# Loading half of the q and k blocks earlier and transposing them in another stage

## The chip, the cores and the metric

The kernel runs on one core of one Trainium2 chip. The time is that of the device, in microseconds, as a median of three runs.

## What is computed

Block-decayed linear attention over q, k, v of shape (4, 8, 768, 64), followed by a two-layer network with the activation h - tanh(h). All numbers are float32.

```python
for b in range(nb):                     # blocks of 64 positions
    intra = einsum('bhic,bhjc->bhij', qb, kb) * Dmask[None]
    intra = einsum('bhij,bhjd->bhid', intra, vb)
    inter = einsum('bhid,bhde->bhie', qb * lam_pow[None], kv_state)
    out[:, :, sl] = intra + inter
    kb_dec = kb * rev_pow[None]
    kv_state = lam_block[None, :, None, None] * kv_state + einsum('bhsd,bhse->bhde', kb_dec, vb)
...
x = out.transpose(0, 2, 1, 3).reshape(3072, 512)
h = x @ w_in                            # (3072, 512) x (512, 2048)
g = h - tanh(h)
return g @ w_out                        # (3072, 2048) x (2048, 512)
```

## The kernel before

The 768 positions are cut into six groups of 128 (`g` = 0 to 5). A group holds one chunk for each of the four batches (`b` = 0 to 3), so 512 tokens. For each group the kernel does the attention of its four chunks, then the two layers on its 512 tokens. The attention of group g + 1 is spread over the layers of group g.

Both layers are done with Strassen-like schemes: seven products in place of eight, called 1 to 7. The first layer (`up(g, u, n)`, line 540) runs over four hidden units `u` of 512 columns. The second layer's products are `down_twice(g, n)` (line 797), here called P1 to P7. Each is cut into seven smaller products again, in the order 1, 2, 6, 5, 7, 3, 4, and each smaller product reads one piece of weights (256 KB) which POOL's queue brings from device memory. The pieces go through a ring of seven buffers (`wb`); four pieces of each P5 go into two extra buffers named `rest`.

From group 2 on, one turn of the outer loop is made of these stages:

- The loop over units, with four first-layer products in each (products 3, 7, 6, 4; the 6 of the first two units are done before), and P1 in its second half.
- P2, then the attention products of chunks 0 and 1 of the next group, then P4 and P5. Inside P5 stand the transposes of chunks 2 and 3.
- P6, the attention products of chunks 2 and 3, P7.
- The inner stage: P3, interleaved with products 1 and 2 of the next group's first layer over all units (`inner_steps`, line 623, lines 637 to 651), then product 5.

For groups 2 to 5 q and k are also loaded in blocks of 32 (`load_blocks`, line 164): for two chunks at a time a tile of q and a tile of k, each by 16 transfers of 32 KB on SyncE's queue. The tiles `q_blk` and `k_blk` come from a pool of four buffers, which the two `rest` tiles share in turn. `att_transpose(g, bs)` (line 354) then does for each chunk two VectorE transposes (line 362) and a product of the transposed q with the powers of the decay (line 373).

SyncE's queue carries, for each of these groups, in this order: the blocks of chunks 0 and 1 (32 transfers), the natural k and v of chunks 0 and 1 (`load_natural`, line 143), the blocks of chunks 2 and 3, the natural k and v of chunks 2 and 3. The last group needs no natural k. The dictionary `hold` makes the first transfer of a group wait for a given instruction. In the kernel before that is the copy on ScalarE of the sixth small product of the inner stage (line 641), two groups ahead of the group that uses the data.

Most operations are placed by a scheduler that follows dependencies and a cost model; those inside `keep_in_program_order` and `tied` keep the order of the code.

Of the kernel before, what the change touches and what calls it, by code (L numbers as in the profile page):

```python
# [24 lines left out]
def kernel(  # L25
# [32 lines left out]
    nc = tc.nc  # L58
# [84 lines left out]
    def load_natural(g, b, names):  # L143
        for name, src, bufs in (("q", q, 2), ("k", k, 3), ("v", v, 4)):
            if name in names:
                if (g, b, name) in ((0, 2, "q"), (0, 3, "q"), (0, 3, "k")):
                    x = opool.tile([128, H, D], F32, name=f"{name}_nat", tag="o")
                else:
                    x = (qpool if name == "q" else io).tile([128, H, D], F32, name=f"{name}_nat", tag=name, bufs=bufs)
                rows = src[b, :, ts(g, BLK), :].rearrange("h s d -> s h d")  # L150
                if name == "q":
                    parts = [(nc.sync, x, rows)]
                else:
                    eng = nc.sync if g > 0 else nc.scalar if b == 0 else nc.gpsimd
                    whole_ = {(0, 1, "k"): nc.scalar, (0, 2, "k"): nc.gpsimd}.get((g, b, name), nc.sync)
                    parts = [(eng, x[ts(1 - t, HALF), 4:8], rows[ts(t, HALF), 4:8]) for t in range(2)]
                    parts.insert(2 * (whole_ is nc.gpsimd), (whole_, x[:, 0:4], rows[:, 0:4]))
                for eng, to, of in parts:
                    op = tc.keep_in_program_order(eng.dma_start(out=to, in_=of))
                    if begin.get(eng) is not None:  # L160
                        wait_for(op, begin.pop(eng))
                raw[g, b][name] = x

    def load_blocks(g, half):

        for name, src in (("q", q), ("k", k)):
            x = late["blk"].tile([128, 2 * NP, BLK // 32, 32], F32, name=f"{name}_blk", tag="blk")
            heads = src[ts(half, 2)].rearrange("b (p j) s d -> j s (b p) d", j=2)
            for r in range(BLK // 32):
                for c in range(4):  # L170
                    op = tc.keep_in_program_order(nc.sync.dma_start(
                        out=x[ts(c, 32), :, r], in_=heads[c // 2, g * BLK + 32 * r:g * BLK + 32 * (r + 1), :, ts(c % 2, 32)]))
                    if g in hold:

                        wait_for(op, hold.pop(g))
            for n in range(2):
                raw[g, 2 * half + n][name + "b"] = x[:, ts(n, NP)]

    def load(n):

        while at["loaded"] < min(n, len(chunks)):
            g, b = chunks[at["loaded"]]
            if g < GB:
                raw[g, b] = {}
                load_natural(g, b, "qkv")
                at["loaded"] += 1
                continue
            for b in range(B):  # L190
                raw[g, b] = {}
            nat = "kv" if g < NG - 1 else "v"

            first = (0, 1, 2) if g == GB else ()
            for b in first:
                load_natural(g, b, nat)
            for half in range(2):
                load_blocks(g, half)
                for b in (2 * half, 2 * half + 1):
                    if b not in first:  # L200
                        load_natural(g, b, nat)
            at["loaded"] += B
# [584 lines left out]
    def sums_twice(g, n):  # L787
# [6 lines left out]
            tied(n in (5, 3, 1, 2) or (g, n) == (1, 6), nc.vector.tensor_tensor(dst, x, y, op=op))  # L794
        low[g, n] = (s1, s2, s3, s4)

    def down_twice(g, n):
        a11, a12, a21, a22 = quarter(g, n)
        s1, s2, s3, s4 = low.pop((g, n))
        y, zw = (("ya", "z") if n in (4, 6) else ("yb", "w")) if g == NG - 1 else ("ya", "z") if n in (5, 3) else ("yb", "w")  # L800
        if n < 3:
            y, zw = "att", "w" if n == 2 else "att"
        y, zw = (bank(x, tag, 4 if tag == "att" else 1) for x, tag in (("y2", y), ("zw", zw)))
        y = y[:, 0:128]
        o = res[g, n] = otile(f"q{n}") if n != 2 else late["pool"].tile([128, 512], F32, name="o11", tag="o11", bufs=1)
        for x, a, dst, keep in ((1, a11, y, o[:, 0:128]), (2, a12, zw[:, 0:128], None), (6, s2, y, o[:, 128:256]),
                                (5, s1, zw[:, 256:384], None), (7, s3, y, o[:, 384:512]), (3, s4, zw[:, 128:256], None),
                                (4, a22, y, o[:, 256:384])):
            wb = piece(g, n, x).rearrange("p m c -> p (m c)")
            for u in range(NU):  # L810
                tied(x == STEPS[-1], nc.tensor.matmul(out=dst, lhsT=a[:, u, :], rhs=wb[:, ts(u, 128)],  # L811
                                                      start=x in (1, 2) and u == 0, stop=u == NU - 1,
                                                      skip_group_check=True))
            if keep is not None:
                nc.scalar.activation(keep, dst, AF.Copy)  # L815
            if x == 2 and n > 2:
                tied(n in (5, 7), nc.vector.tensor_tensor(a12, a12, s2, op=AL.subtract))  # L817
            if x != STEPS[-1]:
                yield

        if n in (6, 2):
            yield
        o5 = o.rearrange("q (i c) -> q i c", i=2)[:, :, 128:256]
        tied(n in (6, 2), nc.vector.tensor_tensor(o5, o5, zw[:, 256:384][:, None, :].to_broadcast([128, 2, 128]), op=AL.add))
        tied(n in (6, 2), nc.vector.tensor_tensor(o[:, 0:256], o[:, 0:256], zw[:, 0:256], op=AL.add))
        if n == 6:
            yield
            tc.keep_in_program_order(nc.vector.tensor_tensor(o, o, res[g, 1], op=AL.add))
            for x in (4, 5):
                tc.keep_in_program_order(nc.vector.tensor_tensor(res[g, x], res[g, x], o, op=AL.add))  # L830
        elif n == 2:
            tc.keep_in_program_order(nc.vector.tensor_tensor(o, o, res[g, 1], op=AL.add))
            store(g, 11, o)
        elif n == 7:
            nc.vector.tensor_tensor(res[g, 4], res[g, 4], o, op=AL.add)
            store(g, 21, res[g, 4])
            nc.vector.tensor_tensor(o, o, res[g, 5], op=AL.add)
            store(g, 22, o)
        elif n == 3:
            nc.vector.tensor_tensor(o, o, res[g, 5], op=AL.add)  # L840
            store(g, 12, o)
        yield

    def every(steps):
        for _ in steps:
            pass
# [181 lines left out]
    for g in range(1, NG):  # L1028
# [7 lines left out]
        for u in range(NU):  # L1036
            if g < GI:
                for n in (2, 6, 5, 7, 1, 4, 3):
                    if n != 1:
                        up(g, u, n)  # L1040
                    elif u + 1 < NU:
                        up(g, u + 1, 1)
                    else:
                        every(p_first)
                    if g == 1 and u < 2 and n == 5:
                        sums_in(u + 2)
                    if n == 6:
                        for p in ((), ((1, 0), (1, 1)), ((1, 2), (1, 3), (2, 0)), ((2, 1), (2, 2)))[u]:
                            fine_pieces(*p)
            else:  # L1050
                up(g, u, 3)
                up(g, u, 7)
                if u + 2 < NU:
                    up(g, u + 2, 6)
                else:
                    next(p_first)
                up(g, u, 4)
                if u + 1 == NU:
                    sums_twice(g, 2)
                if u != 2:  # L1060
                    steps(p_first, (2, 1, 0, 2)[u])
                if not last and u < 2:
                    att_transpose(g + 1, (u,))
                elif not last:
                    att_decays(g + 1, (u - 2,))
            if g == GI - 1 and u + 1 < NU:
                inner_weights(u)
            if not last and u > 1 and g < GI:
                run(p0[u - 2:u - 1])
# [34 lines left out]
        sums_once(g, 21, 21, 11)  # L1104
        sums_twice(g, 6)
        every(p5)
        if not last:
            att_decays(g + 1, (2, 3))
        if twice(g, 7):
# [13 lines left out]
        inner_tokens(g + 1)  # L1123
        sums_twice(g, 3)
        p3, pa, pb, pc = (down_twice(g, 3), *(inner_steps(g + 1, n) for n in INNER))
        for _ in STEPS:
            next(p3)
            next(pa)
            next(pb)
        for p in (pa, pb, p3):  # L1130
            every(p)
        for x in STEPS:
# [40 lines left out]
```

## Time and profile before

| | us |
|---|---|
| median of three runs | 652.08 (651.89 to 652.57) |
| profiled execution | 650.99 |
| its span | 649.2 |
| TensorE busy | 641.8 |
| VectorE busy | 499.2 |
| POOL busy | 242.6 |
| mean rate of transfers | 209 GB/s |

The profile is of one execution. A row of the instructions in order of time holds the start in us from the span's start, the duration, the engine (PE is TensorE, PEld its weight loads, DVE VectorE, ACT ScalarE, POOL GpSimd, SP SyncE), the line, the operation, the tile written and the tiles read, and how many instructions the row merges. A bracket holds the idle time of the engine ahead of it and what released it. One float32 matmul of the code shows as two instructions on TensorE. The granted TensorE clock is 1.00 in every window read.

The stages of group 2 lie at 269.05 to 303.45 (loop over units), 303.45 to about 345.5 (P2 to P7), 345.5 to 370.71 (inner stage). Groups 3 and 4 follow at distances of 101.7 and 101.4 us. Group 1's inner stage is at 245.4 to 269.05, and the last group starts its loop at 572.45.

### The profile page before, as it was taken

What the parts mean: (1) busy time and instruction counts of PE and PEld (TensorE: products, weight loads), DVE (VectorE), ACT (ScalarE), POOL (GpSimd) and SP (SyncE); (2) the same over time, 40 slices, a digit from 0 to 9 for tenths busy, and PEclk for the clock granted to TensorE, in tenths of its full rate; (3) what the DMA queues carried; (4) which work ended last, traced back from release to release, by engine and by line L of the source; (5) the groups of instructions that cost most, each with busy time, mean ns of one, the idle gap of its engine ahead of it and who ended that gap; (6) DMA issues with size and microseconds to landing.
All of it is one profiled execution on the core that took longest, in us unless ns stands there. A gap on an engine that the chain in (4) does not pass through costs nothing.

```text
span 649.2 us, 15718 instructions
## 1 busy us (share of the span) xinstructions
PE 641.8 (99%) x6080; PEld 594.7 (92%) x6080; DVE 499.2 (77%) x969; ACT 250.2 (39%) x513; POOL 242.6 (37%) x418
## 2 busy tenths in 40 slices
PE   8999999999999999999999999999999999999998
PEld 7888888888888999989999989999998999998997
DVE  4467989958999895778986678998477997485873
ACT  3686765523221222543223453213453313264210
POOL 6000136767756335203435302443411354411341
PEclk9999999999999999999999999999999999999999
DMA  9869987988979858958757967775967686712575
GB/s 201 214 168 206 247 244 233 382 252 231 276 191 268 242 181 253 220 118 220 247 174 226 248 134 160 230 253 199 237 140 158 199 274 210 233 67 66 159 247 162
DMA packets 160281, 135.79 MB, mean 209 GB/s; under 512 B 128640, under 2 KB 130944, under 8 KB 160208
## 3 DMA queue, kind: packets, MB, share of 16 engines
q0 software_dynamic: 30496, 97.88, 47.8%
q1 hardware_dynamic: 128096, 36.53, 26.6%
q8 instruction: 48, 0.79, 0.5%
q10 hardware_dynamic: 1616, 0.39, 0.3%
q14 instruction: 25, 0.20, 0.1%
HBM read 110.10 MB, written 24.64 MB: 208 GB/s over the span
## 4 chain that ended last, share of the span: by engine, by line
PE 91%; DVE 4%; DMA 2%; ACT 1%; issue 1%; ACTq 0%; SPq 0%; DVEq 0%
PE y L811 17%; PE y L553 17%; PE zw L811 13%; PE h L870 8%; PE y L637 7%; PE z L553 6%; PE acc L900 4%; PE z L637 3%; DMA k_nat<-in_k_dram 2%; PE sp L387 2%; PE op L462 2%; PE w L637 2%; PE kv L408 1%; PE op L433 1%; PE end L856 1%; PE op L473 1%
## 5 line engine op out<-in xcount | busy, mean ns | idle before, releaser
L696 POOL DMA_DIRECT2D wb<-fine x204 | 110.1, 540 | 244.0 <-PE y L811 160.8
L815 ACT ACTIVATE q<-y 128x128 f32<-128x128 f32 x112 | 31.1, 277 | 143.2 <-PE y L811 141.7
L811 PE MATMUL y<-wb,g 128*128 128x128 f32 x584 | 76.5, 277 | 0.2 <-DVE tt L618 0.2
L811 PEld LDWEIGHTS y<-wb,g 128*128 128x128 f32 x584 | 70.5, 192 | 1.2 <-issue 0.4
L870 PE MATMUL h<-xt,w 128*128 128x256 f32 x256 | 57.8, 382 | 0.4 <-DVE w L325 0.4
L870 PEld LDWEIGHTS h<-xt,w 128*128 128x128 f32 x256 | 47.6, 190 | 7.8 <-DVE w L325 1.1
L811 PE MATMUL zw<-wb,g 128*128 128x128 f32 x368 | 48.9, 276 | 0.0
L561 ACT ACTIVATE th<-g 128x512 f32<-128x512 f32 x40 | 25.2, 630 | 59.9 <-DVE g L579 42.2
L562 DVE TENSOR_TENSOR g<-g,th 128x512 f32<-128x512 f32 x40 | 27.7, 691 | 24.5 <-ACT th L561 24.4
L811 PEld LDWEIGHTS zw<-wb,g 128*128 128x128 f32 x368 | 44.8, 192 | 0.6 <-DVE g L817 0.6
L553 PE MATMUL y<-xt,w 128*128 128x256 f32 x192 | 45.0, 379 | 0.0
L553 PEld LDWEIGHTS y<-xt,w 128*128 128x128 f32 x192 | 36.4, 190 | 5.1 <-ACT g L570 0.2
L553 PE MATMUL z<-xt,ws 128*128 128x256 f32 x160 | 38.8, 381 | 0.1
L553 PE MATMUL y<-tt,w 128*128 128x256 f32 x160 | 38.3, 382 | 0.0
L811 PE MATMUL zw<-wb,s 128*128 128x128 f32 x280 | 37.9, 275 | 0.0
L553 PE MATMUL y<-tt,ws 128*128 128x256 f32 x160 | 37.8, 379 | 0.0
L811 PE MATMUL y<-wb,s 128*128 128x128 f32 x280 | 37.5, 277 | 0.0
L811 PEld LDWEIGHTS zw<-wb,s 128*128 128x128 f32 x280 | 35.2, 192 | 0.4
L811 PEld LDWEIGHTS y<-wb,s 128*128 128x128 f32 x280 | 34.7, 192 | 0.6
L553 PEld LDWEIGHTS y<-tt,w 128*128 128x128 f32 x160 | 29.8, 190 | 4.7 <-DVE g L574 0.5
L900 PE MATMUL acc<-wt,g 128*128 128x256 f32 x144 | 33.5, 382 | 0.4 <-DVE g L906 0.2
L553 PEld LDWEIGHTS y<-tt,ws 128*128 128x128 f32 x160 | 29.8, 190 | 3.7
(215 smaller groups left out, 1446.0 us busy)
## 6 DMA issues: line engine op xcount, KB each, us to landing
wb<-fine POOLq DMA_DIRECT2D x204, 256.0 KB, 3.8
wb<-fine_in POOLq DMA_DIRECT2D x36, 256.0 KB, 4.4
raw<-in_moe_w_out_dram SPq DMA_DIRECT2D x12, 512.0 KB, 6.2
rest<-fine POOLq DMA_DIRECT2D x20, 256.0 KB, 4.6
raw<-in_moe_w_in_dram SPq DMA_DIRECT2D x16, 256.0 KB, 6.2
fine<-f POOLq DMA_DIRECT2D x16, 256.0 KB, 4.8
q_blk<-in_q_dram SPq DMA_DIRECT2D x128, 32.0 KB, 3.4
k_blk<-in_k_dram SPq DMA_DIRECT2D x128, 32.0 KB, 3.5
```

The lines of the kernel that those rows point to most:

```text
L387: tied(g != 1, nc.tensor.matmul(out=sp[j][ts(r, HALF), x:3 + p:2 + p - x, :], lhsT=k0, rhs=qj.rearrange("d (t i) -> d t i", t=2), start=Tr ...
L408: tied(g == 0, nc.tensor.matmul(out=kv[ts(j, 64), n, p, :], lhsT=kd[:, 2 * p + j, :], rhs=vn[:, 2 * p + j, :], start=n == 0 and p == 0, st ...
L462: tied(g == 0, nc.tensor.matmul(out=dst(n, p, j)[:, HALF:BLK], lhsT=vn[:, 2 * p + j, :], rhs=ss[:, j, 2 + p, :], start=g == 0 and n == 0 a ...
L553: nc.tensor.matmul(out=t[:, m, :], lhsT=wt[:, kt, ts(m, 128)], rhs=x[:, kt, :], start=first and m == 0 and kt == 0, stop=kt == 1, skip_gro ...
L561: nc.scalar.activation(th, src, AF.Tanh)
L562: nc.vector.tensor_tensor(dst(c), src, th, op=AL.subtract)
L637: nc.tensor.matmul(out=dst[:, ts(u, 128)], lhsT=a, rhs=b, start=x in (1, 2, 5) and u == 0, stop=True, skip_group_check=True)
L696: nc.gpsimd.dma_start(out=t.rearrange("p m c -> p (m c)"), in_=fine[TWICE.index(n_), SUB.index(x_)].rearrange("p u c -> p (u c)"))
L811: tied(x == STEPS[-1], nc.tensor.matmul(out=dst, lhsT=a[:, u, :], rhs=wb[:, ts(u, 128)], start=x in (1, 2) and u == 0, stop=u == NU - 1, s ...
L815: nc.scalar.activation(keep, dst, AF.Copy)
L870: tied(u == 0, nc.tensor.matmul(out=hm[c][:, m, :], lhsT=w1[u][:, i, a, ts(m, 128)], rhs=xt[0, t][:, i, :], start=m == 0 and i == 0, stop= ...
L900: nc.tensor.matmul(out=acc[n][:, r, :], lhsT=a[:, ts(r, 128)], rhs=b, start=kt == 0 and r == 0, stop=kt == KH - 1, skip_group_check=True)
```

## The change

The blocks of chunks 0 and 1 of groups 3, 4 and 5 are loaded behind P5 two groups ahead. Their first transfer waits for the last ScalarE copy of that P5 (`kept[5]`). The natural loads of the same group take over the wait for the inner stage's copy. The transposes of chunks 0 and 1 of these groups move from the first two units of the loop of the group before into the inner stage two groups ahead, behind its third and fourth step. Group 2's blocks and transposes stay as they were.

```diff
@@ load_natural
                 for eng, to, of in parts:
                     op = tc.keep_in_program_order(eng.dma_start(out=to, in_=of))
+                    if g in hold:
+                        wait_for(op, hold.pop(g))
                     if begin.get(eng) is not None:
                         wait_for(op, begin.pop(eng))
                 raw[g, b][name] = x
+
+    def load_early(g, op):
+
+        for b in range(B):
+            raw[g, b] = {}
+        hold[g] = op
+        load_blocks(g, 0)
 
@@ load
             for b in range(B):
-                raw[g, b] = {}
+                raw.setdefault((g, b), {})
...
             for half in range(2):
-                load_blocks(g, half)
+                if "qb" not in raw[g, 2 * half]:
+                    load_blocks(g, half)
@@ down_twice
             if keep is not None:
-                nc.scalar.activation(keep, dst, AF.Copy)
+                kept[n] = nc.scalar.activation(keep, dst, AF.Copy)
@@ loop over units
-                if not last and u < 2:
-                    att_transpose(g + 1, (u,))
-                elif not last:
+                if not last and u > 1:
                     att_decays(g + 1, (u - 2,))
@@ behind P5
         every(p5)
+        if g + 2 < NG:
+            load_early(g + 2, kept[5])
@@ inner stage
-        for _ in STEPS:
+        for i, _ in enumerate(STEPS):
             next(p3)
             next(pa)
             next(pb)
+            if i in (2, 3) and g + 2 < NG:
+                att_transpose(g + 2, (i - 2,))
```

In the order of instructions this moves, besides the transposes and the waits named, only a few things: in three loops TensorE's z product of the third unit is split after its first two matmuls instead of its first four (one matmul of the code instead of two), the last group but one has a few matmuls of P1 and P2 in another order, and POOL's four transfers into `rest` are issued ahead of four or five pieces of the ring instead of behind them.

More of the change, by code (lines that the diff above doesn't have):

```diff
@@ L795, in sums_twice @@
         low[g, n] = (s1, s2, s3, s4)
+    kept = {}
     def down_twice(g, n):
```

## Prediction

> **What bounds the kernel now.** I read the page first, then a table of windows cut at the stages of groups 2 to 5, then the instructions in order of time in the two places that the change touches, then the transfers.
>
> ```profile
> span 649.2 us, 15718 instructions
> PE 641.8 (99%) x6080; PEld 594.7 (92%) x6080; DVE 499.2 (77%) x969; ACT 250.2 (39%) x513; POOL 242.6 (37%) x418
> PE 91%; DVE 4%; DMA 2%; ACT 1%; issue 1%; ACTq 0%; SPq 0%; DVEq 0%
> ```
>
> TensorE is busy for 641.8 of 649.2 us and carries 91% of the chain. A change that takes no matmul away can only win stalls between matmuls. The windows by stage (PE, PEld, DVE, ACT, POOL busy, clock, DMA share, GB/s) say the same of the three loops over hidden units that lose transposes (groups 2, 3, 4), and of the last group's, which has none:
>
> ```profile
> 269.05:303.45 34.40, 34.29 (x186) 30.66 (x186) 26.86 (x42) 14.78 (x27) 5.37 (x10) 1.00 0.72 153
> 345.47:370.71 25.24, 25.24 (x225) 25.20 (x225) 15.83 (x30) 10.48 (x21) 11.37 (x20) 1.00 0.93 251
> 370.71:404.84 34.13, 34.13 (x187) 30.68 (x186) 26.87 (x42) 14.82 (x27) 5.37 (x10) 1.00 0.66 146
> 472.09:506.29 34.20, 34.20 (x186) 30.67 (x186) 25.51 (x40) 14.45 (x27) 5.36 (x10) 1.00 0.67 156
> 572.45:606.64 34.19, 34.19 (x186) 30.57 (x186) 22.48 (x34) 14.86 (x27) 3.22 (x6) 1.00 0.17 53
> ```
>
> The loops take 34.40, 34.13 and 34.20 us with six to eight more VectorE instructions than the last group's (40 to 42 against 34), which takes 34.19 us. So VectorE there has room already. The second line is the inner stage of group 2: DMA at 0.93, VectorE at 15.8 of 25.2 us.
>
> The instructions of group 2's loop around the second moved transpose show the one stall of size:
>
> ```profile
> 290.61 0.70 DVE L362 STREAM_TRANSPOSE qt<-q_blk 128x512 f32<-128x512 f32 x1
> 291.24 0.67 DVE L362 STREAM_TRANSPOSE kt<-k_blk 128x512 f32<-128x512 f32 x1
> 291.83 0.65 DVE L373 TENSOR_TENSOR qd<-qt,fwd 128x512 f32<-128x512 f32 x1
> 292.40 0.68 DVE L579 TENSOR_TENSOR g<-g,z 128x512 f32<-128x512 f32 x1
> 293.18 1.05 PE L811 MATMUL zw<-wb,s 128*128 128x128 f32 x8
> 293.71 0.58 ACT L529 ACTIVATE z<-g 128x512 f32<-128x512 f32 x1
> 294.34 0.73 PEld L553 LDWEIGHTS z<-xt,ws 128*128 128x128 f32 x4 [0.30 <-ACT z L529]
> 294.34 1.13 PE L553 MATMUL z<-xt,ws 128*128 128x256 f32 x4
> 295.31 1.89 PE L553 MATMUL y<-tt,w 128*128 128x256 f32 x8
> ```
>
> A set of eight 128x128 matmuls takes 0.89 us from its start to the next (341.73 to 342.62, in P7). Here the next begins 1.16 us after 293.18, so 0.27 us is lost: the weight load names its releaser, the seed of z (L529), which waits for L579, which stood behind the transposes. Four 128x256 matmuls take 0.86 us (297.04 to 297.90); from 294.34 to 295.31 is 0.97, so 0.11 more is lost to L574's read.
>
> The inner stage, where the transposes go:
>
> ```profile
> 351.83 0.69 DVE L651 TENSOR_TENSOR g<-g,w 128x512 f32<-128x512 f32 x1 [0.21 <-PE w L637]
> 354.17 10.42 SPq L171 DMA_DIRECT2D q_blk<-in_q_dram  x16
> 358.98 0.69 DVE L648 TENSOR_TENSOR g<-r,y 128x512 f32<-128x512 f32 x1 [6.46 <-PE y L637]
> 363.17 1.95 PE L637 MATMUL y<-tt,w 128*128 128x128 f32 x16
> 364.69 10.65 SPq L171 DMA_DIRECT2D k_blk<-in_k_dram  x16
> ```
>
> VectorE stands idle for 6.46 us in front of L648. The order of instructions of the changed kernel puts both pairs of transposes and both products exactly there, behind the two L651 and ahead of the two L648.
>
> **The change part by part.**
>
> *Taken out of the loop:* per group 2 x (0.70 + 0.67 + 0.65) = 4.0 us of VectorE by duration, about 3.8 us by starts. On the path this is worth only the stalls at the third unit. In group 3 the set before is on time (394.84 to 395.74) and the four z matmuls take 0.95 (395.74 to 396.69): 0.09 lost. Group 4: 497.11 to 498.07, 0.10 lost. What is left without transposes I read from the last group, whose order at this point is the one the changed kernel has in all three (two z matmuls, then y, then six z): 597.47 to 597.91 to 599.67, where 0.43 and 1.73 would do, so 0.04 lost. Gain: (0.38 - 0.04) + (0.09 - 0.04) + (0.10 - 0.04) = 0.45 us. The stall at the fourth unit (0.05 + 0.10 in group 2, 0.17 + 0.10 in the last group) is not the transposes' and stays.
>
> *Put into the inner stage:* 3.8 us of VectorE from 352.5 to 356.3, hidden by the 6.46 us of idle. Group 1 has the same gap: L651 ends at 250.86, L648 starts at 257.31. If that cover were gone, L648 would slip; TensorE feels it when the next use of the same bank, y<-tt,w at 363.17, has to wait for the second L648, which ends at 360.56 now. That is 2.6 us more of cover. Cost: nothing, if the data is there.
>
> *Is the data there?* The early loads wait for the last copy of P5 (L815 at 328.44, 0.28 us, in group 2) and for the buffers, whose last readers, the transposes of the third and fourth chunk, end at 326.7. The SyncE queue is free then: its last transfer of the group before was issued at 316.72, and the next thing on it, k of the first chunk, waits for the inner stage's sixth product as before (354.15). The 32 transfers took 8.79 + 7.98 us to issue in group 3's loop and 10.42 + 10.65 in the inner stage. So the last is issued at 328.7 + 16.8 to 21.1 = 345.5 to 349.8, and lands 1.8 to 7.0 us later (the range of k_blk, median 3.5): 347 to 357, likely 350. Behind k_blk there are still about 3.1 us of VectorE, so nothing moves if it lands by 355.9, and TensorE feels nothing before 358.5. Cost: none, with some 3 us to the worst case.
>
> *Behind them on SyncE:* the natural k and v of the first two chunks go out at 354 instead of 375, the second half of the blocks from about 362 instead of 383. Nothing waits for these early, so this gains nothing, but it keeps the DMA full in the inner stage.
>
> *POOL's queue:* the four `rest` pieces no longer wait for the loop's transposes. They go out near 371 rather than at 397 and 403. The next pieces of the ring are due at 381.8 and are already loaded, so neither cost nor gain.
>
> *The price that the trace doesn't show directly: the pieces' transfers beside the early loads.* P6 of the same group now shares the DMA with the blocks. Time from issue to landing of the pieces, in 326 to 346 and in 346 to 371:
>
> ```profile
> DMA to landing us min/median/max: 2.7/3.6/4.6
> DMA to landing us min/median/max: 3.2/4.3/5.8
> ```
>
> The second has block loads beside it and is the nearest row. The tightest piece is P6's last: issued at 328.70, first used at 333.84, so 5.1 us are there; the ones before it were issued before any block moves, and P7's are all in by the time the attention products (334.7 to 339.8) end. At 4.3 us there is no stall; at 5.8 us, 0.7 per group. The blocks' own work also bounds it: 16815 packets cost 45.2% of 34 us in the loop of group 3, 0.23 us per block transfer; some six can be moving before that piece lands. Below nothing it can't be, since the piece was on time. I take 0.05 per group, 0.15 in all, and keep 0 to 0.7 for the range. In the inner stage the natural loads replace blocks; the tightest there is P3's last piece, issued at 355.59 and used at 362.28, 6.7 us against a worst of 5.8: nothing.
>
> [...]
>
> **Sum.** -0.45 + 0.15 = -0.3 us. The profiled execution took 650.99 us (span 649.2 plus 1.8 around it) and would take 650.7. It is 1.1 us under the median of the runs, 652.08; the same 0.3 off the median is 651.8.
>
> **Rivals.**
> (a) *Pieces late in P6* (slower). The early blocks put P6's last piece past 5.1 us. For: DMA is at 0.90 from 330 to 335 already. Against: only one piece is exposed, and 4.3 us is the median beside such loads. At 5.8 us: 3 x 0.7 = 2.1, less the gain 0.45, gives 653.7. It eats the gain from a landing time of 5.3 us (3 x 0.15) and is slower by over 0.2% from 5.7. Chance 0.13.
> (b) *Transposes wait for k_blk.* If it lands after 358.5, each microsecond more costs one in each of three groups; at 360, 3 x 1.5 - 0.45 = +4 us, 656. Against: needs an issue pace slower than any seen. Chance 0.04.
> (c) *All stalls of the three loops go* (faster), the fourth unit's too: 0.53 + 0.25 + 0.33 = 1.1 us, 651.0. Against: the last group, without transposes, still loses 0.31. Chance 0.08.
> (d) *It does not do what it says*: blocks wait behind something on SyncE and arrive as late as before, which is (b). Included there.
>
> **How the numbers follow.** Forecast, 0.75: 651.8, with 651.2 to 652.5 from the unknown piece cost and the spread of runs (651.89 to 652.57). 0.2% is 1.3 us, about what a measurement of this kernel can tell from no change. Case (c) falls just short of it: 0.05 of it counts as faster for what its terms leave open, and 0.01 of the forecast. Slower are 0.10 of (a) and all of (b). So faster 0.06, same 0.80, slower 0.14. The range 650.9 to 653.3 takes in (c) and the nearer half of (a).
>
> **What would show it.** Right: in the inner stages VectorE runs L362 from about 352.5 with no long wait for q_blk or k_blk, and L648 starts when the product ends; the loops of groups 2, 3, 4 take 34.0 to 34.15 us; P6's sets stay 0.89 us apart; the total stays with TensorE. Wrong: VectorE idle in front of L362 on a block transfer, POOL or TensorE waiting for wb, P5 to P7 longer than before, or a loop below 33.9 us.

## The result: 0.33% slower, and the profile after

The changed kernel takes 653.99 us (median of 20 runs, 651.66 to 656.83) against 652.09 us for the kernel before in the same session (20 runs, 649.74 to 653.25). The ratio is 1.0033, with a 95% interval of 1.002 to 1.0046, so 1.3 to 3.0 us more. Its profiled execution took 654.62 us, 3.6 us more than the one of before (650.99 us). The forecast was 651.8 us, within a range that ended at 653.3.

The page of the changed kernel:

```profile
span 652.8 us, 15715 instructions
PE 642.1 (98%) x6080; PEld 594.9 (91%) x6080; DVE 499.9 (77%) x969; ACT 250.8 (38%) x513; POOL 242.4 (37%) x418
PE 89%; DVE 5%; DMA 3%; issue 2%; ACT 1%; POOL 0%; ACTq 0%; DVEq 0%
```

The work is the same: TensorE's busy time is 642.1 us (before: 641.8). The span is 3.6 us longer, so TensorE stands still more. "issue", time in which an engine waited for nothing that the profile shows, rose from 1% to 2% of the chain.

The windows by stage, in the order of those shown of before (the loop that began at 269.05, group 2's inner stage, the three other loops):

```profile
270.50:304.57 34.07, 34.07 (x187) 30.59 (x186) 23.31 (x36) 14.78 (x27) 5.37 (x10) 1.00 0.55 130
346.84:372.08 25.24, 25.24 (x226) 25.20 (x225) 19.29 (x35) 10.47 (x21) 11.36 (x20) 1.00 1.08 282
372.08:406.16 34.08, 34.08 (x187) 30.60 (x186) 23.31 (x36) 14.82 (x27) 5.35 (x10) 1.00 0.56 130
475.04:509.16 34.12, 34.11 (x185) 30.52 (x185) 22.42 (x34) 14.79 (x27) 5.35 (x10) 1.00 0.48 119
575.78:609.97 34.19, 34.18 (x187) 30.60 (x186) 22.48 (x34) 14.85 (x27) 3.23 (x6) 1.00 0.18 53
```

The three loops went from 34.40, 34.13 and 34.20 us to 34.07, 34.08 and 34.12, a gain of 0.46 us. The inner stage takes 25.24 us as before, with 3.5 us more VectorE work in it. Both are what the change was for.

VectorE in group 2's inner stage, where the transposes now stand:

```profile
353.21 0.69 DVE L661 TENSOR_TENSOR g<-g,w 128x512 f32<-128x512 f32 x1 [0.21 <-PE w L647]
353.81 0.70 DVE L372 STREAM_TRANSPOSE qt<-q_blk 128x512 f32<-128x512 f32 x1
357.64 0.71 DVE L372 STREAM_TRANSPOSE kt<-k_blk 128x512 f32<-128x512 f32 x1 [3.12 <-DMA k_blk<-in_k_dram]
360.07 0.65 DVE L383 TENSOR_TENSOR qd<-qt,fwd 128x512 f32<-128x512 f32 x1
360.64 1.30 DVE L658 TENSOR_TENSOR g<-r,y 128x512 f32<-128x512 f32 x2
```

VectorE waits 3.12 us for the last k block, which landed at 357.6. TensorE does not notice: its products in this stage start 1.38 us after those of before at 353.83 and still 1.38 us after at 364.55.

**Where the time went.** I compared the start of each stage on TensorE in the two traces. Group 1's attention of chunks 2 and 3 (between P6 and P7) takes 1.83 us more, group 3's 1.61 us more, and P7 of group 2 loses 0.24 us. That is 3.68 us. P6, which carried the prediction's risk, changed by 0.00, 0.02 and 0.01 us. The chain of waits of the changed kernel shows the two large ones (start, us, what):

```profile
237.45 1.57 issue
...
441.43 1.33 issue
```

The instructions of TensorE there, in order of time. First the changed kernel, then the kernel before at the same place:

```profile
236.15 1.10 PE L472 MATMUL op<-ss,v_nat 128*64 128x64 f32 x32
237.18 0.27 PE L483 MATMUL op<-ss,v_nat 64*64 64x64 f32 x1
239.01 0.69 PE L483 MATMUL op<-ss,v_nat 64*64 64x64 f32 x31 [1.57 <-issue]
```

```profile
236.52 1.10 PE L462 MATMUL op<-ss,v_nat 128*64 128x64 f32 x32
237.56 0.69 PE L473 MATMUL op<-ss,v_nat 64*64 64x64 f32 x32
```

One instruction of L483 runs, and then TensorE stands before the other 31, which need nothing that the first did not need. From the start of the one to the start of the next it is 1.83 us, of which 1.57 show as idle; stands are counted from start to start below. No semaphore released it. In the kernel before the 32 run in one piece.

What is missing there is the instructions themselves. The page lists a queue for instructions in both kernels, and it moved the same in both:

```profile
q8 instruction: 48, 0.79, 0.5%
```

48 transfers of 0.79 MB are 16 KB each. The trace has 12452 records of TensorE's instructions, so 259 for each transfer by this count. TensorE stood after its instructions number 4289 (group 1) and 8641 (group 3). These are 16 x 256 + 193 and 33 x 256 + 193: a whole multiple of 256 apart, so the same place in a transfer, 17 transfers apart. Such a place is called a border here. The small loss in group 2 stands after number 6593 = 25 x 256 + 193. The transfers are short, and they end close to their use (numbered from 0; us; the last column is from the transfer's end to the first instruction behind the border):

| transfer | kernel | start | end | TensorE goes on behind the border | after the end |
|---|---|---|---|---|---|
| 15 (group 1) | before | 234.20 | 235.64 | 237.56, no stand | 1.92 |
| 15 | changed | 236.11 | 237.53 | 239.01, stood 1.83 | 1.48 |
| 24 (group 2) | before | 337.47 | 338.39 | 342.18, no stand | 3.79 |
| 24 | changed | 341.15 | 342.22 | 343.57, stood 0.25 | 1.35 |
| 32 (group 3) | before | 436.86 | 438.15 | 439.86, no stand | 1.71 |
| 32 | changed | 439.80 | 441.12 | 442.76, stood 1.55 | 1.64 |

Wherever TensorE stood at one of these three borders, in any kernel of this study, it went on 1.2 to 1.6 us after the end of the transfer. So the kernel before had only 0.3 to 0.7 us to spare at transfer 15 and 0.1 to 0.5 at transfer 32. The need isn't sharp: in two traces a transfer ended 1.43 and 1.46 us ahead of use and TensorE didn't stand (number 15 in experiment 4, number 32 in experiment 10).

The changed kernel's transfers start late by TensorE's own count as well. When transfers 15, 24 and 32 begin, the kernel before still has 240, 219 and 220 of the instructions ahead of the border to start, the changed kernel 64, 39 and 89. The attention products are where instructions run out fastest: 360 to 389 of them in 4.6 to 5.0 us, against 16 in 0.89 us in a set of eight products and their weight loads. And the DMA engines are full there now. Windows of 234 to 239 us (before, then changed; busy PE, PEld, DVE, ACT, POOL, clock, DMA share, GB/s). The share adds up the times of all packets that start in the window and divides by the time of 16 engines, so it can exceed 1:

```profile
234.00:239.00 5.00, 5.00 (x177) 4.69 (x170) 4.93 (x13) 1.98 (x6) 0.51 (x1) 1.00 0.37 114
```

```profile
234.00:239.00 5.00, 3.45 (x122) 3.07 (x111) 4.93 (x11) 1.28 (x4) 0.14 (x1) 1.00 1.03 215
```

### The profile page after: what moved, and what is told of

Its sections match the earlier page's. It is cut to its first block, busy times and chain, and to the rows that moved or that the text cites. A ratio compares the mean times of both kernels' runs of the same rounds, so it can differ in the third digit from the quotient of the medians.

```text
span 652.8 us, 15715 instructions
## 1 busy us (share of the span) xinstructions
PE 642.1 (98%) x6080; PEld 594.9 (91%) x6080; DVE 499.9 (77%) x969; ACT 250.8 (38%) x513; POOL 242.4 (37%) x418
## 4 chain that ended last, share of the span: by engine, by line
PE 89%; DVE 5%; DMA 3%; issue 2%; ACT 1%; POOL 0%; ACTq 0%; DVEq 0%
PE y L563 17%; PE y L823 17%; PE zw L823 12%; PE h L882 8%; PE y L647 7%; PE z L563 6%; PE acc L912 4%; PE z L647 3%; PE op L472 2%; PE sp L397 2%; PE w L647 2%; PE kv L418 1%; PE op L443 1%; PE op L483 1%; DMA q_nat<-in_q_dram 1%
```

## The experiments

Three theories were tested. **T**: the transposes in the inner stage cost the time. **W**: the weight pieces (`wb`) come late beside the early blocks. **C**: TensorE's instruction transfers come late beside the early blocks.

The time of a whole run holds something else besides. Ahead of 40 us, long before any early load, the traces of these kernels (number 7, which alters the start, apart) differ by up to 3.7 us: from 0.6 us quicker than the kernel before in number 5 to 3.1 us slower in number 9. Most of it is stands behind instructions 449 and 705, which are also 193 beyond a multiple of 256: 0.14 us in all in the kernel before, up to 2.8 at one border in the others. How much of a ratio below is due to this is not known, so the stands at the three later borders say more about the early loads than the ratios do.

**1. Only the early loads.** The transposes go back into the loop; the loads stay behind P5.

```diff
-                if not last and u > 1:
+                if not last and u < 2:
+                    att_transpose(g + 1, (u,))
+                elif not last:
...
-            if i in (2, 3) and g + 2 < NG:
-                att_transpose(g + 2, (i - 2,))
```

> Only the loads are early (behind P5); the transposes of chunks 0 and 1 are back in the loop over units. Theory C (TensorE's instructions arrive late): the block transfers between P6 and P7 hold back the 16 KB transfers on the instruction queue while the attention products use instructions fastest, so TensorE stands for about 1.5 us in some of groups 1 to 3, with no releaser. Then this kernel is as slow as the changed one, 1.5 to 3 us over the kernel before. Rival T (the transposes in the inner stage cost the time): within 0.5 us of the kernel before. Rival W (the weight pieces of P6 land late): slow too, but with TensorE waiting on wb in P6 instead of standing without a releaser in the attention products.

Measured: 655.38 us, ratio 1.0045 (1.0025 to 1.0065). It stands at the same two instructions, 1.16 us after 4289 and 0.69 us after 8641, and 0.53 us after 6593. The loops are as long as before. So T falls: the stands are there without the moved transposes. Another 0.48 us is lost in P6 of group 2, away from a border. The profile names VectorE's L628 as the releaser, but two pieces of weights land at 336.88 and 338.03 there, and the products that read them begin 0.14 us later, at 337.02 and 338.17. So W holds too, for a small part.

**2. The same loads, but behind the attention products of chunks 2 and 3.** Transposes in the loop as in 1.

```diff
-        if g + 2 < NG:
-            load_early(g + 2, kept[5])
...
-            att_out(g + 1, (2, 3))
+            op = att_out(g + 1, (2, 3))
+        if g + 2 < NG:
+            load_early(g + 2, op)
```

> The early loads wait for the last copy of the attention output of chunks 2 and 3 (some 11 us later than in the changed kernel, in P7 and the inner stage); the transposes are in the loop over units, as before. Theory C: no stand of TensorE over 1 us in the attention products, time within 0.6 us of the kernel before. Rival T: the same, so this one only counts beside a1. Rival W: the same, since P7's pieces have more room. If the natural loads that now come earlier cost the time, this kernel is slow like the changed one.

Measured: 653.32 us, ratio 1.001 (0.9994 to 1.0026). No stand at any of the three borders; transfers 15, 24 and 32 end 2.5, 3.4 and 2.7 us before they are needed. The same block transfers, begun behind the attention products, leave TensorE alone there. The time by itself doesn't show it: the median is 1.5 us over the kernel before, where C expected at most 0.6. In the profiled execution 1.9 us are lost ahead of 40 us.

**3. The changed kernel again**, for comparison on the same chip.

> The changed kernel, unaltered, for a second profile and times on the same chip as the others: 1.3 to 3 us over the kernel before. Theory C: one to three stands of about 1.5 us without a releaser in the attention products of groups 1 to 3, not in the same groups in each execution, since they depend on when an instruction transfer is asked for and what is queued then. Rivals T and W: the same places in each execution.

Measured: 655.21 us, ratio 1.0044 (1.0025 to 1.0062). It stands 1.37 us after 4289 and 1.69 us after 8641; the three loops again gain 0.33, 0.05 and 0.08 us. C's expectation that the groups would change from one execution to the next missed: they are the same, because the borders lie there. In P6 of group 2 a piece lands at 337.65, its products begin at 337.79, and 0.35 us is lost.

**4. Split:** 8 of the 32 transfers behind P5, 24 behind the attention products, transposes in the inner stage.

```diff
-            load_early(g + 2, kept[5])
+            blocks_in = load_early(g + 2, kept[5])
+            for _ in range(EARLY):          # EARLY = 8
+                next(blocks_in)
...
-            att_out(g + 1, (2, 3))
+            op = att_out(g + 1, (2, 3))
+        if g + 2 < NG:
+            hold[g + 2] = op
+            for _ in blocks_in:
+                pass
```

> The changed kernel with 8 of the 32 early transfers behind P5 and 24 behind the attention products of chunks 2 and 3; transposes in the inner stage (those of k behind the second y addition, by the scheduler). Theory C: no stand over 1 us in the attention products and the gain in the loops is kept, so -0.5 to +0.3 us against the kernel before, unless the k transposes wait for their blocks (last issue near 353 us, landing near 357, wanted at 362). Rival T: as slow as the changed kernel. Rival W: between, since 8 transfers still lie beside P6.

Measured: 653.39 us, ratio 1.0016 (1.0001 to 1.0031). With a quarter of the early transfers one stand is left, 0.42 us after 8641. The loops keep their gain, but the time missed the expected -0.5 to +0.3 us: the interval is 0.1 to 2.0 us over the kernel before.

**5. Extra transfers to device memory.** The kernel before, with 32 transfers of the same blocks (packets of 128 bytes) behind P5, written to device memory and not used.

```diff
+        if g + 2 < NG:
+            extra(g, kept[5])   # 32 x nc.sync.dma_start(out=spare[...], in_=heads[...])
```

> The kernel before, plus 32 extra transfers on SyncE's queue behind P5 of groups 1 to 3 with the shapes and sources of the early blocks (packets of 128 B), into device memory that nobody reads. Blocks, transposes and natural loads stay as before. Theory C: TensorE stands without a releaser for 0.7 to 1.8 us in the attention products of groups 1 and 3, at the same two instruction counts as in the changed kernel, and the time is 1.5 to 4 us over the kernel before. If the early loads hurt by their effect on buffers or the order of the kernel's own loads: no change.

Measured: 653.23 us, ratio 0.9999 (0.9974 to 1.0024), no stand at the three borders. C's expectation missed.

**6. The same with long runs** (32 transfers of 32 KB, 864 packets in place of the 7330 of number 5 between 225 and 248 us).

```diff
+                e = nc.sync.dma_start(out=spare[g - 1, y], in_=moe_w_out[ts(32 * (g - 1) + y, 16), 0:256])
```

> As the one with small packets, with the same number of transfers and bytes, but in runs of 2048 B, so 16 packets instead of 256 in each transfer. If it is the number of small packets that holds back the instruction transfers (C with packets): no stand over 0.6 us, time within 0.5 us of the kernel before. If it is the number of transfers on the queue (C with transfers): as slow as with small packets.

Measured: 652.94 us, ratio 0.9998 (0.9981 to 1.0016), no stand at the three borders. In both, transfer 15 ends 1.94 and 1.97 us before it is needed, as in the kernel before (1.92). So transfers behind P5 do not make TensorE stand merely by being issued there. They are not without effect: in number 5 transfer 24 began when 66 instructions were left ahead of its border (219 in the kernel before), and ended 1.74 us before it was needed, just in time. Why blocks into on-chip buffers put the instruction transfers off more is not settled; the DMA share from 234 to 238 us was 0.73 in number 5 against 1.11 in the changed kernel. That left C without a test that adds the load alone, which experiment 9 makes.

**7. The instruction stream shifted by half a transfer.** The changed kernel with 32 more idle products, 128 instructions in the trace, near the start.

```diff
-    idle_products(8, True)
+    idle_products(40, True)
```

> The changed kernel with 32 more idle products on TensorE at the start, where it waits for the first loads: 128 more instructions as the trace counts them, which is half of one 16 KB instruction transfer. All later work meets the borders between transfers half a transfer earlier. Theory C: the stands leave groups 1 and 3 (there they now look as group 2 did) and one of about 1 to 2 us comes up in group 2, at a count of 193 modulo 256; in all one stand instead of two, so 1 to 2 us faster than the changed kernel, 0 to 2 over the kernel before. Any theory by which the transfers hurt the data of the attention: stands stay in groups 1 and 3, time as the changed kernel.

Measured: 663.06 us, ratio 1.0148 (1.012 to 1.0175). About 7 us of that is lost ahead of 40 us, among it a stand of 2.75 us at a border. So the expected time, at most 2 us over the kernel before, missed by far. What counts is the place: in group 1, where the border has moved out of the attention's last products, the stand is gone, and group 2, where the changed kernel lost 0.24 us, now has one. Group 1, then group 2:

```profile
244.27 0.69 PE L483 MATMUL op<-ss,v_nat 64*64 64x64 f32 x32
```

```profile
344.58 0.86 PE L472 MATMUL op<-ss,v_nat 128*64 128x64 f32 x22
347.89 0.56 PE L472 MATMUL op<-ss,v_nat 128*64 128x64 f32 x10 [2.44 <-issue]
```

It stands 2.66 us after instruction 6593, again 193 beyond a multiple of 256, now inside a run of equal products. Nothing in the data sets the 22nd and the 23rd instruction apart; the border of the instruction transfer lies between them. Group 3's stand was expected to go; it moved behind the attention instead, to 8897 = 34 x 256 + 193 (1.99 us).

More time goes behind the stand in group 2. The granted TensorE clock there is 0.50 from 349.10 to 350.80 us and 0.54 to 352.40 (the mean of that execution is 0.997), the first eight products of P7 take 2.08 us instead of 1.16, and P7 loses 1.49 us more. Behind the changed kernel's stands of 1.83 and 1.55 us the clock stays at 1.00 (239 to 246 and 443 to 448 us). That the stand brought the clock down is not shown.

**8. All 32 transfers behind the attention products, transposes in the inner stage.** This is number 4 with `EARLY = 0`, and the candidate to beat both kernels.

> The changed kernel with all 32 early transfers behind the attention products of chunks 2 and 3, transposes in the inner stage where the scheduler puts them. Theory C: no stand over 0.6 us in the attention products. The gain in the loops (0.45 us) can be kept, or lost again to k transposes that wait for blocks whose last issue is near 362 us: -0.5 to +1 us against the kernel before.

Measured: 652.04 us, ratio 0.9994 (0.9974 to 1.0014), no stand at the borders. The loops gain 0.33, 0.05 and 0.09 us, as in the changed kernel, but two of the three inner stages lose 0.41 and 0.33 us, where blocks arrive while the inner stage needs its pieces (TensorE waits 0.17 us for `wb<-fine` at 256.06). It is no faster than the kernel before as far as this can be measured.

**9. The early load alone.** The kernel before, with the 32 block transfers of the next group but one issued a first time behind P5 into the same buffers, and again at the old place. On every compute engine the order of instructions is that of before, and the output too.

```diff
+        if g + 2 < NG:
+            first_pass(g + 2, kept[5])   # the 32 transfers of load_blocks(g + 2, 0)
```

> The kernel before, with one thing added: the 32 block transfers of group g+2's first two chunks are issued a first time behind P5, into the same buffers, and again at the old place. The order on every compute engine and of every other transfer is that of before; the output is the same. If TensorE stands because its instruction transfers come late under the blocks (theory C): the DMA share in 234-239 us rises from 0.37 to over 0.9, the transfers number 15 and 32 start half a transfer later than in before (lag 1.4 or more against 0.8 to 0.9), TensorE stands with no releaser at instruction 4289 or 8641, 0.5 to 1.9 us each, and the time is 1.002 to 1.0065 of before, as with the early loads alone. If instead something else of the change is the cause (the blocks that are gone from the inner stage, the natural loads that move up, the rest pieces that go out earlier): no stand at these two instructions and a time within 0.2%.

Measured: 655.89 us, ratio 1.0056 (1.0035 to 1.0077). Its window and its instructions:

```profile
234.00:239.00 5.00, 4.96 (x129) 4.42 (x127) 4.85 (x14) 1.13 (x5) 1.61 (x3) 1.00 1.13 261
```

```profile
240.49 0.27 PE L492 MATMUL op<-ss,v_nat 64*64 64x64 f32 x1
241.59 0.69 PE L492 MATMUL op<-ss,v_nat 64*64 64x64 f32 x31 [0.83 <-issue]
```

The DMA share is 1.13, and TensorE stands 1.09 us after 4289 and 1.62 us after 8641, at the product where the changed kernel stands. When transfers 15 and 32 begin, 111 and 73 instructions are left ahead of the border. The early transfers by themselves make the stands; neither their absence from the inner stage nor the earlier natural and `rest` loads is needed for them. One of the second loads comes late too, for 0.34 us in group 3's loop.

**10. The early load alone, in long runs.** As number 9, but the first set reads q and k in runs of 2 KB: as many transfers and bytes, and 1010 packets on SyncE's queue between 225 and 248 us instead of 6804.

```diff
-                    out=x[ts(c, 32), :, r], in_=heads[c // 2, ..., :, ts(c % 2, 32)]
+                    out=x[ts(n // 2, 16), ts(n % 2, NP)].rearrange("p a r e -> p (a r e)"), in_=runs[ts(16 * g + n, 16)]
```

> As the kernel that loads twice, but the added first set reads q and k in runs of 2 KB (16 rows for each transfer) into the same buffers; as many transfers (32) and as many bytes (32 KB each), 16 packets for each instead of 256. What is loaded by them is overwritten by the second set, so the output is the same. If the many small packets are what delays TensorE's instruction transfers: DMA share in 234-239 us near before's 0.37 to 0.7, lag of number 15 and 32 at most 1.2, no stand, time within 0.2% of before. If the bytes, or that so many transfers go out from SyncE at all, were enough: stands at 4289 or 8641 as in the kernel that loads twice, and 1.002 to 1.0065.

Measured: 653.05 us, ratio 1.0019 (1.0002 to 1.0035), between the two expectations.

```profile
239.05 0.27 PE L491 MATMUL op<-ss,v_nat 64*64 64x64 f32 x1
240.47 0.69 PE L491 MATMUL op<-ss,v_nat 64*64 64x64 f32 x31 [1.15 <-issue]
```

It stands 1.41 us in group 1 and not at all in group 3. The number of packets is therefore not the whole cause: the same bytes in a seventh of the packets can still delay a transfer of instructions, though in the profiled execution they did so in one group of two.

## Why the prediction was wrong

**The gain was right.** Forecast: 0.34, 0.05 and 0.06 us from the three loops, 0.45 in all. Measured: 0.33, 0.05 and 0.08, so 0.46, and the same again in experiments 3, 4 and 7.

**The inner stage was right, with less to spare than said.** The transposes cost TensorE nothing there. The blocks were issued in 20.5 us, inside the 16.8 to 21.1 given. The last landed at 357.6. The first was issued 1.2 us later than the prediction assumed (329.86 for 328.7), so on its scale that is 356.4: not the likely 350 but near the late end of the range, 357. VectorE stood 3.12 us for it.

**The pieces in P6 (0.05 for each group, 0.15 in all) cost less than that.** P6 changed by 0.00, 0.02 and 0.01 us. The transfers to `wb` did become slower, as the prediction feared, and by more than its worst case of 5.8 us:

```profile
DMA to landing us min/median/max: 2.8/4.9/6.6
```

That is 327 to 347 us of the changed kernel; before, the median there was 3.6. P6's last piece still came in time: it landed at 334.64 and was used at 334.98. The rival "pieces late in P6" gave 653.7 us, close to the measured 653.99, but that is luck. Pieces did come late in experiments 1 and 3, in group 2 alone, for 0.48 and 0.35 us, inside the 0 to 0.7 kept for them; the stands at the borders are a different wait and a larger one.

**What failed is the step on the price of the early loads beside P6 and P7.** It counted one kind of transfer that could be late, the weight pieces, and passed over the attention products because no piece is needed in them. The page listed a second kind, the 48 transfers of queue q8. The step should have asked what else moves by DMA between 329 and 350 us, when it is needed, and how much it has to spare. The table above shows that the trace of before held the answer: transfers 15 and 32 landed 1.92 and 1.71 us ahead of use. That 1.2 to 1.6 us of this is needed shows there only faintly: behind instruction 3521 = 13 x 256 + 193 the next starts 0.26 us after the one ahead of it, at 212.33, 1.50 us after its transfer ended.

The missed term is 3.68 us in the profiled execution; with the gain of 0.46 and the loss in P6 of 0.03 it makes +3.25. The rest of the 3.6 us of span is a start that was 0.39 us quicker and an end of group 4 and 5 that was 0.82 us slower. Of that end, 0.56 lies ahead of group 5's first layer, and it does not follow the change: the same place ranges from -0.44 us (experiments 1, 5 and 9) to +0.55 (number 6, which has no early blocks in on-chip buffers). One more border lies there, 10689 = 41 x 256 + 193, with a stand of 0.58 us in the changed kernel and 0.54 in number 6. The other part was not looked into. The medians differ by less (1.3 to 3.0 us). How long TensorE stands, at these borders and at the start of a run, differs from one execution to the next: 1.83 and 1.55 us in one profile of the changed kernel, 1.37 and 1.69 in another.

**What stays open.** The records give a transfer's first movement, not when it was asked for, so by what way the blocks hold the instruction transfers back is not shown. Shown is that the blocks cause it (experiments 1, 2 and 9) and that the stand sits at the border (experiment 7). Why the same bytes in long runs made one stand in place of two (experiment 10: 1.41 us, and none in group 3), and transfers to device memory none (experiments 5 and 6), is open as well.

## What to carry to other kernels

Before a load is moved to a place where the DMA engines look idle, list everything that moves by DMA there, the engines' own instructions included, and ask when each is needed and what it has to spare. In this kernel instructions ran out fastest where many small products stand together (360 to 389 in 4.6 to 5.0 us, against 16 in 0.89 us), and 32 block transfers beside such a stretch made TensorE stand for 1.83 and 1.55 us, though no data of the stretch depended on them. The stands at the borders, without a releaser, recurred at the same count of TensorE's instructions modulo 256 (193), and at the three borders of the table TensorE went on 1.2 to 1.6 us after a transfer of instructions had ended: where a stand has no releaser, count, before looking for a semaphore. And a whole-run difference of 1 or 2 us is best checked border by border: stands of the same kind at the start of the run came to 0.14 us in the kernel before and to as much as 2.8 us at one border in the others.

## What the hardware showed

- Each of the 48 instruction transfers moves 16 KB. They took 0.92 to 1.44 us at the three borders in the kernel before and the changed one. The trace has 12452 records of TensorE's instructions, and its stands at these borders lie whole multiples of 256 apart. TensorE, where it stood at one of them, went on 1.2 to 1.6 us after the transfer had ended.
- Block transfers into on-chip buffers put off such a transfer by some 2 us (number 15: from 234.20 to 236.11, in a stage that began 0.37 us sooner).
- 32 transfers of the same size, issued at the same place and written to device memory, caused no stand there, with packets of 128 bytes (experiment 5) and with long runs (experiment 6) alike.
- Adding 32 idle products at the start moved a stand of 1.83 us out of group 1, and one of 2.66 us into group 2 (experiment 7).
- Behind that stand of 2.66 us the granted TensorE clock was 0.50 to 0.54 for 3.3 us; behind stands of 1.83 and 1.55 us it was 1.00.
